# VectorE subtracts a session's upper parts one session later, behind the copy that opens it

## The chip, the cores and the metric

One core of a Trainium2 chip runs the whole program: the matrix engine (TensorE, PE in the rows), VectorE (DVE), ScalarE (ACT), GpSimd (POOL), which here issues transfers, and SyncE (SP), which issues the others. The metric is the time of one execution in microseconds, the median of several runs.

## The reference

Attention through 49 agents for four batches of 12480 tokens, and behind it a two-layer network with squared relu over all 49920 rows:

```
a2k     = softmax(scale * agents @ k.T)        # per batch, 49 x 12480
agent_v = a2k @ v                              # 49 x 128
x       = softmax(scale * q @ agents.T) @ agent_v
h       = maximum(x @ w_in, 0)                 # 49920 x 2048
out     = (h * h) @ w_out                      # 49920 x 128
```

## The kernel before

The kernel never forms x. For each batch it multiplies agent_v with w_in into a table (`aw_hi` and a small rest `aw_ex`), so that a block of at most 504 tokens needs only its softmax weights (`w`, `x`), which are multiplied with the table to give h. The 2048 columns of h are 16 chunks of 128.

**Sessions.** The main loop runs over sessions: 199 that take one block of 504 (or, at a batch's end, 384) tokens and 8 of the 16 chunks, and two of 4 chunks at the very end. A block is two sessions. In session s, TensorE first makes the 8 chunks of h (`first`: 8 matmuls with the table and 8 narrow ones, `x<-` in the rows, which run four at a time on 19 rows). They fill all eight banks of its accumulator memory, four called x and four called y; the tags A and B change places from session to session. ScalarE rectifies 7 banks into a tile `r` of fp32, VectorE the eighth (`rectified`, `r<-A` or `r<-B` on DVE). ScalarE squares `r` in two halves of four chunks (`squared`), and behind each half GpSimd issues a transfer that writes the half's fp16 rounding, the upper part `g_hi` (line 1039).

**Two sessions later** (`LAG`), TensorE multiplies these squares back with w_out (`second`): per chunk `g_hi` with the lower and the upper part of w_out (16 matmuls), and then `g_lo` with the upper part (8 matmuls, `g_lo,wo_hi`). `g_lo = r - g_hi` is the lower part. VectorE makes it, in two subtractions of 128x2016 a session (`rest`, called by `low_parts`). All 24 matmuls add into one bank, x[0] of the running session, and VectorE copies the sums out (`copied_out`, `ob<-`), scaled, adding two sessions to a block's result. I call this the copy. A copy of session n's sums comes at the end of session n+2. The next session needs the bank back for the first of its y chunks: its narrow matmul into that bank waits for the copy.

**What sets the order.** Every instruction of TensorE, ScalarE and VectorE is chained to the one issued before it on its engine, so each engine runs in the order of the program's text. Work for the softmax weights of later blocks, and for keys and values of the next batch, is cut into steps that are called at named phases of a session: L, P, A1, D, E, A3. P holds TensorE's steps; A1 and A3 ScalarE's; D and E VectorE's. In D stand the maximum and the subtraction of a block's scores (`m`, `e`) or the cast of its turned weights (`w`), in E the normalising group (three on `z`, one on `e`), or `pp`, or steps on `mx` and `d` for keys and values.

**Around the change**, VectorE's order within session s is: the eighth bank's rectification, phase D, the first subtraction for session s-1, the copy of session s-2, phase E, the second subtraction for s-1. The function `ending` runs what is left of `second` and the copy; `low_parts` calls it between its two subtractions. At the start (s = 0), nine instructions that split the last quarter of w_out's parts (`makes`, `keeps`: tiles `last`, `t`, `wo_hi`, `wo_lo`) stand behind phase D of session 0. At the end, `late_parts` rounds and subtracts for the two sessions of four chunks, on VectorE alone.

Of the kernel before, what the change touches and what calls it, by code (L numbers as in the profile page):

```python
# [29 lines left out]
LAG = 2  # L30
# [3 lines left out]
WIDE = 512  # L34
# [16 lines left out]
def agent_attention_relu2(ctx: ExitStack, tc: tile.TileContext, qT, kT, v, agT, w_in, w_out, outT):  # L51
# [4 lines left out]
    FF = w_in.shape[1]  # L56
# [15 lines left out]
    def queued(issue, eng, *args, **kw):  # L72

        with tc.issue_after(chain[eng]) if eng in chain else ExitStack():
            ins = issue(*args, **kw)  # L75
        chain[eng] = ins.ins
        return ins
# [75 lines left out]
    def decoded(dec, raw, t):  # L153
        low, high = raw[:, :, 0], raw[:, :, 1]
        n = raw.shape[1]
        dve.scalar_tensor_tensor(
            out=t, in0=high, scalar=0xC0000000, in1=t, op0=ALU.bitwise_and, op1=ALU.bitwise_or
        )

        rest = dec[:, 1, :] if n == 512 and not hasattr(dec, "tile") else dec.tile([P, n], F32, name="rest", bufs=4)  # L160
        dve.tensor_single_scalar(rest.bitcast(U32), t, 0xFF800000, op=ALU.bitwise_and)
        dve.scalar_tensor_tensor(out=rest, in0=low, scalar=2.0**-52, in1=rest, op0=ALU.mult, op1=ALU.mult)
        return t.bitcast(F32), rest

    def kept(at, t, rest):
        n = t.shape[1]
        if at < FF:
            pool.tensor_add(win[:, at : at + n], t, rest)
            if at + n == FF:
                pool.tensor_mul(squares, win, win)  # L170
            return iter(())
        c = slice((at - FF) // C, (at - FF + n) // C)
        hi, lo = (x[:, c, :].rearrange("p c d -> p (c d)") for x in (wo_hi, wo_lo))
        return kept_later(hi, lo, t, rest) if at > FF else scaled(hi, lo, t, rest)
# [306 lines left out]
    def place(k):  # L481
        b, i = divmod(k // HALF, HB)
        return b * NB + i // 2, i % 2, k % HALF * SET

    def width(k):
        return REST if k // HALF % HB == HB - 1 else G
# [58 lines left out]
    def rest(lo, r, hi, at, n):  # L545
        x = slice(at % SET, at % SET + n)
        queued(nc.vector.tensor_sub, nc.vector, lo[:, x, :], r[:, at : at + n, :], hi[:, x, :])
# [4 lines left out]
    def lower(k):  # L552
        return late.tile([P, SET, G], F16, name="g_lo", bufs=LOWS)[:, :, : width(k)]

    def second(k, m, o):
        _, _, at = place(k)
        his, los = parts.pop(k)
        todo = [(w, c, his[c // SET][:, c % SET, :]) for c in range(m * SET) for w in (wo_lo, wo_hi)]
        for x, lo in enumerate(los):
            todo += [(wo_hi, x * SET + c, lo[:, c, :]) for c in range(SET)]  # L560
        last = len(todo) - 1
        for i, (w, c, y) in enumerate(todo):
            queued(nc.tensor.matmul, nc.tensor, o, w[:, at + c, :], y, start=(i == 0), stop=(i == last))
            yield

    def copied_out(k, m, o):
        g, j, at = place(k)
        if at == 0:
            whole[0] = late.tile([P, G], F32, name="ob", bufs=3)[:, : width(k)]
            queued(nc.vector.tensor_scalar_mul, nc.vector, whole[0], o, state[g // NB]["rho"])  # L570
        else:
            queued(
                nc.vector.scalar_tensor_tensor, nc.vector, out=whole[0], in0=o, scalar=state[g // NB]["rho"],
                in1=whole[0], op0=ALU.mult, op1=ALU.add,
            )
        if at + m * SET == NCH:
            t = g // NB * N + (g % NB * 2 + j) * G
            nc.sync.dma_start(outT[:, t : t + width(k)], whole[0])
# [28 lines left out]
    def step(gen):  # L607

        with ExitStack() as es:
            for ins in behind:  # L610
                es.enter_context(tc.issue_after(ins))
            return next(gen, None)

    def run(gen):
        for _ in gen:
            pass
# [51 lines left out]
    with tc.tile_pool(name="pre", bufs=PRE) as pre, tc.tile_pool(name="raws", bufs=RAW) as raws_in, tc.tile_pool(name="dec", bufs=4) as dec:  # L668
# [47 lines left out]
        def makes(at):  # L716
            raws[at] = decoded(*raws[at])

        def keeps(at):
            return kept(at, *raws.pop(at))  # L720
# [19 lines left out]
        for i in range(NK):  # L740
# [7 lines left out]
            s = sp.tile([P, 512], F32, name="s")[:, :n]  # L748
# [8 lines left out]
            if i in (0, 4, 8):  # L757
                at = i // 4 * WIDE
# [39 lines left out]
        z = small.tile([P, 1], F32, name="z0")  # L798
# [96 lines left out]
    sessions, starts, at = [], [], 0  # L895
# [43 lines left out]
    def allowed(name, s, gate):  # L939
        if gate == "told":  # L940
            return s == todo["told"]
        if gate == "any":
            return s >= todo["start"]
        if gate == "values":
            todo["told"] = s + 2 + s % 2
        todo["room"] = room(s if gate == "blocks" else todo["told"])
        return todo["room"] > 0

    def phase(name, s):
        for gen in plan.pop((s, name), ()):  # L950
            step(gen)
        while todo["next"]:
            (at, lead, *gate), since = todo["next"]
            if at != name or s < since + lead or gate and not allowed(name, s, *gate):
                break
            said = step(todo["gen"])
            todo["next"] = said and (said, s)
# [7 lines left out]
            rounded(hi, r, i, 2)  # L965
            rest(lo, r, hi, i, 2)

    def low_parts(z, first):
        k, n = sessions[z]
        r, his = made.pop(z)  # L970
        los = [lower(k) for _ in range(n)]
        parts[k] = his, los
        phase("D", z + 1)
        for x in range(n):
            if x:
                run(first)
                phase("E", z + 1)
            rest(los[x], r, his[x], x * SET, SET)

    def resting(n):  # L980
        for _ in range(n):
            pe.matmul(desk["at"][BLOCKS][:, :P], ones, ones, start=True, stop=True)

    def ending(s, work, o):
        run(work)
        if s >= LAG:
            copied_out(*sessions[s - LAG], o)
        yield

    made, x = {}, None  # L990
    todo["end"] = starts[NB]
    for s in range(len(sessions) + LAG):
        k, m = sessions[s] if s < len(sessions) else (total, 0)
        if s == LAG:
            behind = [chain[eng] for eng in (nc.tensor, nc.sync, nc.scalar, nc.vector, nc.gpsimd)]
        if s in starts and s // 2 and starts.index(s) % NB == 0:
            assert not todo["next"]
            b = starts.index(s) // NB
            if b + 1 < B:
                todo.update(gen=background(b + 1), done=0, start=s, end=starts[(b + 1) * NB])  # L1000
                todo["next"] = (step(todo["gen"]), s)
        phase("L", s)

        tags = "AB" if s % 2 == 0 else "BA"
        x = Banks(tags[0])
        o = x[0][:, : width(sessions[s - LAG][0])] if s >= LAG else None

        if m:
            r = held("r", F32, m, k)
            made[s] = r, []  # L1010
            if s:
                x, y = first(k, m, x, lambda: Banks(tags[1]))
                rectified(r, x, 0)
            else:
                x, _ = first(k, 1, x, None)
                rectified(r, x, 0)
                for n in (2, 3):
                    run(table(n, (n - 1,)))
                y, _ = first(k + 1, 1, Banks(tags[1]), None)
        desk["at"] = x  # L1020
        work = second(*sessions[s - LAG], o) if s >= LAG else iter(())
        for _ in range(LEAD):
            next(work, None)
        if s and s < LAG:
            resting(IDLE[0])
        phase("P", s)
        if s and s < LAG:
            resting(IDLE[1])
        if m == 2:
            rectified(r, y, SET, TAKEN[s] if s < LAG else 1)  # L1030
        if s == 0:
            phase("D", s)
            makes(2 * FF - WIDE)
            for at in (FF + 2 * WIDE, FF + 3 * WIDE):
                run(keeps(at))
        for x in range(m if m == 2 else 0):
            squared(r, x * SET, SET)
            made[s][1].append(upper(x, k))
            nc.gpsimd.dma_start(made[s][1][x], r[:, x * SET : (x + 1) * SET, :])  # L1039
            if x == 0:  # L1040
                phase("A1", s)
        if m != 2:
            phase("A1", s)
        if m == 1:
            for n in (0, 2):
                squared(r, n, 2)
        ended = ending(s, work, o)
        if s - 1 in made:
            low_parts(s - 1, ended)
        phase("D", s)  # L1050
        run(ended)
        phase("E", s)
        if m == 1:
            late_parts(s)
        phase("A3", s)
        todo["more"]()
# [36 lines left out]
```

## Time and profile before

| | us |
|---|---|
| median of 3 runs | 1760.4 (1758.71 to 1764.08) |
| the profiled execution, its own time | 1757.98 |
| its span | 1755.8 |
| TensorE busy | 1691.0 (96%) |
| VectorE busy | 1478.8 (84%) |
| ScalarE busy | 1499.9 (85%) |
| share of full clock that TensorE was granted | 0.995 |

A busy engine is one whose instructions overlap any moment; matmuls are pipelined, so TensorE's busy time counts their modelled tails too. A wait in the rows is idle time of one engine just before an instruction, with what released it in square brackets. In a timeline row the first number is the start, the second the duration, both in us; `x8` means that eight equal instructions are merged.

### The profile page before, as it was taken

The numbers are of one execution on the slowest core, as the hardware profiler recorded it, in microseconds if no ns is written. First come the engines' busy times: TensorE is split into PE (matmuls) and PEld (weight loads), VectorE is DVE, ScalarE is ACT, GpSimd is POOL, SyncE is SP. The second block draws the span as 40 slices with busy tenths as digits, with TensorE's granted clock in tenths as the row PEclk, the third lists the DMA queues.
The fourth block names the chain that finished last, engine by engine and source line by source line (L and its number), as shares of the span: only waits on it lengthen the run. The fifth ranks groups of instructions, "written<-read, shape, count | busy, mean of one in ns | idle before, by whom it ended". The sixth has DMA issues, their size and how long they took to land.

```text
span 1755.8 us, 40344 instructions
## 1 busy us (share of the span) xinstructions
PE 1691.0 (96%) x16731; PEld 788.0 (45%) x16731; DVE 1478.8 (84%) x1602; ACT 1499.9 (85%) x2063; POOL 233.4 (13%) x422
## 2 busy tenths in 40 slices
PE   7799999999999999999999999999999999999998
PEld 3444444444444444444444444444444444444444
DVE  6888878888887788888888788888888888888887
ACT  4688888888888888988889789888888999999996
POOL 2211111111111111111111111111111111111111
PEclk9999999999999999999999999999999999999999
DMA  9678888889788888888779887888778888787776
GB/s 380 182 172 197 211 185 186 200 193 205 161 172 183 210 185 193 193 201 187 160 166 189 191 192 168 178 208 187 153 158 167 177 170 186 165 175 166 155 156 122
DMA packets 116439, 324.03 MB, mean 185 GB/s; under 512 B 13648, under 2 KB 48160, under 8 KB 116256
## 3 DMA queue, kind: packets, MB, share of 16 engines
q0 software_dynamic: 62688, 203.71, 60.7%
q1 hardware_dynamic: 53568, 117.74, 20.5%
q8 instruction: 131, 2.15, 0.5%
q14 instruction: 52, 0.43, 0.1%
HBM read 80.97 MB, written 25.56 MB: 61 GB/s over the span
## 4 chain that ended last, share of the span: by engine, by line
PE 50%; issue 33%; DMA 5%; DVE 5%; POOL 4%; ACT 3%; SPq 0%; POOLq 0%; ACTq 0%; DVEq 0%
PE A L75 26%; PE B L75 23%; DMA g_hi<-r 4%; POOL g_hi L1039 4%; ACT r L75 2%; DVE g_lo L75 1%; DMA ahead<-in_kT 1%; DVE ob L75 1%; PE h L75 1%; PE o L75 0%; DVE e L75 0%; DVE r L75 0%; DVE z L75 0%; POOLq L1039 0%; SPq L75 0%
## 5 line engine op out<-in xcount | busy, mean ns | idle before, releaser
L75 DVE TENSOR_TENSOR g_lo<-r,g_hi 128x2016 f16<-128x2016 f32 (+2 forms) x402 | 892.2, 2220 | 67.5 <-DMA g_hi<-r 66.8
L75 ACT ACTIVATE r<-r 128x2016 f32<-128x2016 f32 (+2 forms) x402 | 742.6, 1916 | 1.3 <-DVE r L75 1.3
L75 ACT ACTIVATE r<-B 128x504 f32<-128x504 f32 (+1 forms) x698 | 359.4, 611 | 137.1 <-PE B L75 136.9
L75 PEld LDWEIGHTS <-wo_hi 128*128 128x128 f16 x3200 | 313.1, 98 | 354.2 <-issue 16.1
L75 ACT ACTIVATE r<-A 128x504 f32<-128x504 f32 (+1 forms) x699 | 360.2, 614 | 67.3 <-PE A L75 67.2
L1039 POOL DMA_DIRECT2D g_hi<-r x398 | 213.7, 537 | 1453.7 <-ACT r L75 1366.3
L75 PE MATMUL A<-g_hi,wo_lo 128*128 128x504 f16 (+1 forms) x804 | 303.0, 377 | 1.5 <-issue 0.8
L75 PE MATMUL A<-g_hi,wo_hi 128*128 128x504 f16 (+1 forms) x804 | 302.0, 376 | 0.0
L75 PE MATMUL B<-g_hi,wo_lo 128*128 128x504 f16 (+1 forms) x796 | 298.0, 374 | 0.6 <-ACT r L75 0.6
L75 PE MATMUL B<-g_hi,wo_hi 128*128 128x504 f16 (+1 forms) x796 | 297.6, 374 | 0.0
L75 PEld LDWEIGHTS <-aw_hi 128*128 128x128 f16 x1600 | 140.4, 98 | 215.5 <-issue 78.8
L75 PEld LDWEIGHTS <-wo_lo 128*128 128x128 f16 x1600 | 156.6, 98 | 171.0 <-issue 6.9
L75 PE MATMUL A<-w,aw_hi 128*128 128x504 f16 (+1 forms) x800 | 219.1, 376 | 2.8 <-DVE r L75 2.8
L75 PE MATMUL B<-w,aw_hi 128*128 128x504 f16 (+1 forms) x800 | 220.2, 378 | 1.6 <-DVE aw_hi L75 1.6
L75 PE MATMUL A<-g_lo,wo_hi 128*128 128x504 f16 (+1 forms) x804 | 186.4, 374 | 6.3 <-issue 5.4
L75 PE MATMUL B<-g_lo,wo_hi 128*128 128x504 f16 (+1 forms) x796 | 184.1, 374 | 0.0
L75 DVE TENSOR_SCALAR ob<-A,rho 128x504 f32<-128x504 f32 (+1 forms) x100 | 73.7, 737 | 82.3 <-PE A L75 54.8
L75 DVE SCALAR_TENSOR_TENSOR ob<-B,rho,ob 128x504 f32<-128x504 f32 (+1 forms) x100 | 73.4, 734 | 36.3 <-PE B L75 33.3
L75 PE MATMUL B<-x,aw_ex 19*128 19x504 f16 (+1 forms) x800 | 77.9, 376 | 18.5 <-DVE ob L75 17.8
L75 PE MATMUL A<-x,aw_ex 19*128 19x504 f16 (+1 forms) x800 | 77.0, 375 | 5.2 <-DVE ob L75 5.2
L75 PEld LDWEIGHTS <-aw_ex 19*128 19x128 f16 x1600 | 28.1, 92 | 119.6 <-issue 119.1
L75 DVE CAST w<-B 98x504 f16<-98x504 f32 (+1 forms) x97 | 65.3, 673 | 10.7 <-ACT r L75 10.2
(192 smaller groups left out, 1004.3 us busy)
## 6 DMA issues: line engine op xcount, KB each, us to landing
g_hi<-r POOLq DMA_DIRECT2D x384, 504.0 KB, 7.0
qt<-in_qT SPq DMA_DIRECT2D x48, 504.0 KB
out_T<-ob SPq DMA_DIRECT2D x96, 252.0 KB
vt<-in_v SPq DMA_DIRECT2D x36, 512.0 KB
kt<-in_kT SPq DMA_DIRECT2D x36, 512.0 KB
x<-w SPq DMA_DIRECT2D x384, 18.7 KB
ahead<-in_kT SPq DMA_DIRECT2D x12, 512.0 KB
ahead<-in_v SPq DMA_DIRECT2D x12, 512.0 KB
```

The source lines that it names most:

```text
L75: ins = issue(*args, **kw)
L1039: nc.gpsimd.dma_start(made[s][1][x], r[:, x * SET : (x + 1) * SET, :])
```

## The change

`low_parts` loses its second argument and the calls between its subtractions. It is called two sessions after the session whose parts it makes, right after the first chunks of the running session are issued, instead of one session after, in front of phase D. `ending` is gone: phase D, then phase E, then the rest of `second` and the copy. The splitting of w_out's last quarter moves from session 0 to session 1, behind phases D and E.

```diff
-    def low_parts(z, first):
+    def low_parts(z):
         k, n = sessions[z]
         r, his = made.pop(z)
         los = [lower(k) for _ in range(n)]
         parts[k] = his, los
-        phase("D", z + 1)
         for x in range(n):
-            if x:
-                run(first)
-                phase("E", z + 1)
             rest(los[x], r, his[x], x * SET, SET)
...
-    def ending(s, work, o):
-        run(work)
-        if s >= LAG:
-            copied_out(*sessions[s - LAG], o)
-        yield
...
         desk["at"] = x
+        if s - LAG in made:
+            low_parts(s - LAG)
         work = second(*sessions[s - LAG], o) if s >= LAG else iter(())
...
         if s == 0:
             phase("D", s)
-            makes(2 * FF - WIDE)
-            for at in (FF + 2 * WIDE, FF + 3 * WIDE):
-                run(keeps(at))
...
-        ended = ending(s, work, o)
-        if s - 1 in made:
-            low_parts(s - 1, ended)
         phase("D", s)
-        run(ended)
         phase("E", s)
+        if s == 1:
+            makes(2 * FF - WIDE)
+            for at in (FF + 2 * WIDE, FF + 3 * WIDE):
+                run(keeps(at))
+        run(work)
+        if s >= LAG:
+            copied_out(*sessions[s - LAG], o)
         if m == 1:
             late_parts(s)
```

No instruction is added or removed. TensorE, ScalarE and GpSimd keep their order row for row; SyncE's transfers of weights change places with a neighbour here and there; VectorE's order changes.

**A session in the steady part**, VectorE, before, from one copy (`ob`) over the next to the one after. The first subtraction stands in front of the copy, the normalising group and the second subtraction behind it:

```order
L75 TENSOR_SCALAR r<-A_2658 128x504
L75 CAST w_2697<-B_2649 98x504
L75 TENSOR_TENSOR g_lo<-r,g_hi_2607 128x2016
L75 SCALAR_TENSOR_TENSOR ob<-B_2646,rho_785,ob 128x504
L75 TENSOR_REDUCE z<-e 126x8
L75 TENSOR_SCALAR z<-z 126x8
L75 RECIPROCAL z<-z 126x8
L75 TENSOR_TENSOR e<-e,z 126x392
L75 TENSOR_TENSOR g_lo<-r,g_hi_2612 128x2016
L75 TENSOR_SCALAR r<-B_2746 128x504
```

And now:

```order
L75 TENSOR_SCALAR r<-A_2654 128x504
L75 CAST w_2695<-B_2645 98x504
L75 TENSOR_REDUCE z<-e 126x8
L75 TENSOR_SCALAR z<-z 126x8
L75 RECIPROCAL z<-z 126x8
L75 TENSOR_TENSOR e<-e,z 126x392
L75 SCALAR_TENSOR_TENSOR ob<-B_2642,rho_785,ob 128x504
L75 TENSOR_TENSOR g_lo<-r,g_hi_2607 128x2016
L75 TENSOR_TENSOR g_lo<-r,g_hi_2612 128x2016
L75 TENSOR_SCALAR r<-B_2742 128x504
```

The first subtraction (of the same tile, g_hi_2607) went behind the copy, and the group on `z` in front of it.

**The start**, VectorE, sessions 0 to 2, before: the splitting of w_out stands ahead of the group on `z` and of session 1's rectification (`r<-A`), the subtractions for session 0 right behind phase D's `e`:

```order
L75 SCALAR_TENSOR_TENSOR wo_lo<-last,omega 128x512
L75 TENSOR_REDUCE z<-e 126x8
...
L75 TENSOR_SCALAR r<-A_910 128x504
L75 TENSOR_TENSOR pp<-e,pp 126x8x49
L75 TENSOR_REDUCE m<-B_900 126x8
L75 TENSOR_TENSOR e<-B_900,m 126x392
L75 TENSOR_TENSOR g_lo<-r,g_hi_892 128x2016
```

And now:

```order
L75 TENSOR_SCALAR r<-A_901 128x504
L75 TENSOR_TENSOR pp<-e,pp 126x8x49
L75 TENSOR_REDUCE m<-B_891 126x8
L75 TENSOR_TENSOR e<-B_891,m 126x392
L75 SCALAR_TENSOR_TENSOR last<-raw_last,last 128x512
...
L75 SCALAR_TENSOR_TENSOR wo_lo<-last,omega 128x512
L75 TENSOR_TENSOR g_lo<-r,g_hi_883 128x2016
```

The nine splitting instructions now stand between phase D of session 1 and the subtractions for session 0.

**The end**, VectorE, before: `g_lo<-r,g_hi_21003` and `21006` are the subtractions for the last session of eight chunks, `g_hi_21081` belongs to the first of the two late ones:

```order
L75 TENSOR_TENSOR g_lo<-r,g_hi_21003 128x4x384
L75 SCALAR_TENSOR_TENSOR ob<-B_21032,rho_16109,ob 128x504
L75 TENSOR_TENSOR g_lo<-r,g_hi_21006 128x4x384
L75 CAST g_hi_21081<-r 128x2x384
L75 TENSOR_TENSOR g_lo<-r,g_hi_21081 128x2x384
...
L75 TENSOR_SCALAR ob<-A_21087,rho_16109 128x384
```

And now:

```order
L75 SCALAR_TENSOR_TENSOR ob<-B_21028,rho_16107,ob 128x504
L75 CAST g_hi_21077<-r 128x2x384
L75 TENSOR_TENSOR g_lo<-r,g_hi_21077 128x2x384
...
L75 TENSOR_TENSOR g_lo<-r,g_hi_21003 128x4x384
L75 TENSOR_TENSOR g_lo<-r,g_hi_21006 128x4x384
L75 TENSOR_SCALAR ob<-A_21083,rho_16107 128x384
```

Both subtractions went behind the copy and behind the four instructions of the first late session.

## Rows read from the trace of the kernel before

**Rows 1.** Page: busy us, share of the span, instructions.

```profile
PE 1691.0 (96%) x16731; PEld 788.0 (45%) x16731; DVE 1478.8 (84%) x1602; ACT 1499.9 (85%) x2063; POOL 233.4 (13%) x422
```

**Rows 2.** Waits of TensorE: total us, times, longest us.

```profile
PE B L75 <- DVE ob L75: 17.8, 24, 1.2
...
PE A L75 <- DVE ob L75: 5.2, 6, 1.2
```

**Rows 3.** Waits of VectorE, same columns.

```profile
DVE g_lo L75 <- DMA g_hi<-r: 66.8, 54, 2.7
...
DVE aw_lo L75 <- ACT aw_hi L75: 17.0, 10, 2.7
```

**Rows 4.** Timeline of VectorE, 214 to 233 us: start, duration, instruction, wait.

```profile
214.56 0.74 DVE L75 TENSOR_SCALAR ob<-A,rho 128x504 f32<-128x504 f32 x1 [1.20 <-PE A L75]
...
221.89 2.26 DVE L75 TENSOR_TENSOR g_lo<-r,g_hi 128x2016 f16<-128x2016 f32 x1 [2.71 <-DMA g_hi<-r]
224.07 0.73 DVE L75 SCALAR_TENSOR_TENSOR ob<-B,rho,ob 128x504 f32<-128x504 f32 x1
...
232.83 0.74 DVE L75 TENSOR_SCALAR ob<-A,rho 128x504 f32<-128x504 f32 x1 [1.59 <-ACT pp L75]
```

**Rows 5.** Timeline of VectorE, 1042 to 1061 us, the same pair of sessions.

```profile
1042.87 0.74 DVE L75 TENSOR_SCALAR ob<-A,rho 128x504 f32<-128x504 f32 x1 [2.07 <-PE A L75]
...
1046.81 0.68 DVE L75 CAST w<-B 98x504 f16<-98x504 f32 x1
...
1050.58 0.74 DVE L75 SCALAR_TENSOR_TENSOR ob<-B,rho,ob 128x504 f32<-128x504 f32 x1
1051.24 0.55 DVE L75 TENSOR_REDUCE z<-e 126x8 f32<-126x392 f32 x1
...
1052.82 2.25 DVE L75 TENSOR_TENSOR g_lo<-r,g_hi 128x2016 f16<-128x2016 f32 x1
1054.98 0.68 DVE L75 TENSOR_SCALAR r<-B 128x504 f32<-128x504 f32 x1
...
1059.72 0.74 DVE L75 TENSOR_SCALAR ob<-A,rho 128x504 f32<-128x504 f32 x1 [1.90 <-issue]
```

**Rows 6.** Timelines of TensorE and ScalarE, 1042 to 1051 us.

```profile
1042.67 1.01 PE L75 MATMUL B<-w,aw_hi 128*128 128x504 f16 x4
...
1044.05 0.38 PE L75 MATMUL A<-x,aw_ex 19*128 19x504 f16 x4
...
1048.68 1.86 PE L75 MATMUL B<-g_lo,wo_hi 128*128 128x504 f16 x8
...
1047.56 3.71 ACT L75 ACTIVATE r<-r 128x2016 f32<-128x2016 f32 x2
```

**Rows 7.** Timelines of VectorE and ScalarE at the start, 76 to 97 us.

```profile
76.28 0.68 DVE L75 SCALAR_TENSOR_TENSOR last<-raw_last,last 128x512 uint32<-128x512 uint32 x1
...
91.20 0.67 DVE L75 TENSOR_SCALAR r<-B 128x504 f32<-128x504 f32 x1
...
93.89 2.25 DVE L75 TENSOR_TENSOR g_lo<-r,g_hi 128x2016 f16<-128x2016 f32 x1
96.06 0.73 DVE L75 TENSOR_SCALAR ob<-A,rho 128x504 f32<-128x504 f32 x1
...
77.31 0.52 ACT L75 ACTIVATE e<-e 126x392 f32<-126x392 f32 x1
...
80.08 1.92 ACT L75 ACTIVATE r<-r 128x2016 f32<-128x2016 f32 x1
```

**Rows 8.** Timelines of VectorE and TensorE at the end, 1742 to 1752 us.

```profile
1742.94 1.75 DVE L75 TENSOR_TENSOR g_lo<-r,g_hi 128x1536 f16<-128x1536 f32 x1
...
1746.28 1.46 PE L75 MATMUL A<-g_lo,wo_hi 128*128 128x384 f16 x8
...
1748.37 0.55 DVE L75 CAST g_hi<-r 128x768 f16<-128x768 f32 x1
...
1751.29 0.61 DVE L75 SCALAR_TENSOR_TENSOR ob<-B,rho,ob 128x384 f32<-128x384 f32 x1
```

## The prediction

> **What bounds the kernel now.** I read the page's busy times first: TensorE is busy for 1691.0 us, 96% of the span [rows 1]. So only TensorE's own waits can be won back, and the next view is the list of what it waits for. The first cause behind the start is the copy of sums: 17.8 us in 24 waits and 5.2 us in 6, the longest 1.2 us [rows 2], together 23.0 us in 30. The reader is to see that these are not one wait per session but 30 in 200 sessions. Why these 30? VectorE's list answers: 54 times, 66.8 us in all, it stood before a subtraction until the transfer of an upper part had landed [rows 3]. VectorE runs in order, so the copy queued behind that subtraction stood too.
>
> A pair of sessions shows it. From the copy at 214.56 to the next at 224.07 pass 9.51 us, because the first subtraction waited 2.71 us for its transfer; the copy after that starts at 232.83, 8.76 us later [rows 4]. The same two kinds of session without a harmful wait take 7.71 and 9.14 us [rows 5]. The first copy of the pair was therefore 9.51 - 7.71 = 1.80 us late, and the pair lost 18.27 - 16.85 = 1.42 us. Two things follow. TensorE forgives a copy that is up to 1.80 - 1.42 = 0.38 us late: undisturbed, the narrow matmul that needs the bank starts at 1044.05 [rows 6], 0.44 us after the copy's end at 1043.61 [rows 5]. And such a wait costs more than the list says: the longest there is 1.2 us [rows 2], and this one cost 1.42. I take 0.2 us more per wait, since a matmul's modelled tail covers part of the gap.
>
> **What the change does to a steady session.** It moves subtractions, and adds none. Between two copies VectorE now runs both subtractions, the eighth bank, phase D, phase E, and the next copy. Nothing of this waits for a fresh transfer: in the slow pair the awaited transfer had landed at 221.89, 2.18 us before the copy at 224.07 [rows 4]. With that copy on time (1.80 earlier, 222.27) and the subtraction 0.66 us behind it (copy to next instruction, 1050.58 to 1051.24 [rows 5]), it would start at 222.93, still 1.04 us after the landing, and this was the longest of the 54 waits. So I cost the transfer's wait at nothing, with 1.04 us of cover.
>
> *Does TensorE get the lower parts in time?* Counted from a copy's start C = 1042.87 [rows 5]: the first subtraction starts at C + 0.66 and takes 2.25, ready at C + 2.91; the second starts 2.16 after the first (1052.82 to 1054.98) and is ready at C + 5.07. TensorE takes the lower parts at 1048.68 [rows 6], C + 5.81, the second four matmuls 0.9 us later (half of the eight's 1.86). Cover 2.9 and 1.6 us: nothing.
>
> *Does the next copy come in time?* The tightest session is the one with a cast in D and the group on `z` in E: 50 of the 201 stretches between copies in the new order. Its sum, from starts to next starts where the rows have them: copy 0.66, two subtractions 2 x 2.16, eighth bank at most 0.68, cast at most 0.68, group 1052.82 - 1051.24 = 1.58 [rows 5]: 7.92 us. TensorE needs 7.71, so the copy is 0.21 late at most, inside the 0.38 that is forgiven: nothing, but the cover is only 0.17 us. These instructions start 0.08 or 0.09 us before their forerunners have ended (a subtraction of 2.25 is followed after 2.16, a copy of 0.74 after 0.66 [rows 5]). The Trainium skill, page "VectorE: DVE Perf Modes", section "Terms", says that the pipe is flushed after every VectorE operation and the next cannot issue before it is empty; added up end to end, the durations of the same rows would give some 8.2 us a session, and 50 sessions would lose about 0.1 us each. The trace does not agree: it shows the overlap, and I take 7.92.
>
> *What of the gain stays away?* Where VectorE waits for ScalarE's part of a new table (`aw_lo`, 17.0 us in 10 waits [rows 3]), the copy stays late if a normalising group now stands in front of it as well. I leave 1.2 us of gain to these, three waits of 0.4. Bounds: 0, and 3 us if three copies stay as late as the longest.
>
> Steady sum: 30 waits, 23.0 us, plus 30 x 0.2 = 6.0, less 1.2, less 0.5 for one that lies at the start: **-27.3 us**. Lower bound of the gain, the list alone less 3: 20. Upper: 29.
>
> **The start.** The nine splitting instructions move behind VectorE's phase D of session 1, ahead of session 0's subtractions. VectorE's work up to these subtractions is the same, now with two waits in it: the `z` group comes at 76.28 and needs the exponential that ScalarE ends at 77.31 + 0.52 = 77.83, 1.55 us; and `pp` needs a cast that ScalarE can only begin after its square, at 80.08 + 1.92 = 82.00, and that takes about 0.5 (my estimate, from the exponential of the same tile, 0.52): 82.5, where VectorE would arrive at 77.83 + 1.58 + 3 x 0.6 = 81.2: 1.3 us. The stretch that ended at 91.20 ends at 94.05; then eighth bank, cast and group, 93.89 - 91.20 = 2.69 as before, and the copy at 96.74 instead of 96.06 [rows 7]. **+0.7 us**, since the next session's narrow matmul waits for this copy. TensorE gets session 1's banks earlier than before, but now waits for the lower parts, so I credit nothing. Bounds: -2, if the earlier banks carry through, and +4, if TensorE after this idling runs slowly for some us.
>
> **The end.** The subtractions for the last session of eight chunks stood before and behind the copy that ends at 1742.94; now both follow it, and the four instructions of the first late session stand between (they take 1751.29 - 1748.37 = 2.92 us, as the second late session's). VectorE: 1742.94 + 2.92 + 2 x 1.7 = 1749.26; TensorE needs that second lower part, which it took from 1746.28 on; its last four matmuls take 0.7 (half of 1.46), the copy 0.5, the last late session 2.92: 1753.4 where it was 1751.29 [rows 8]. **+2.1 us.** Nothing hides it, as every step waits for the one before; bounds 1.5 and 3.
>
> **Sum:** -27.3 + 0.7 + 2.1 = -24.5 us. Against the profiled execution: 1757.98 - 24.5 = 1733.5. The median of the runs shown is 1760.4, 2.4 us above that execution, so 1735.9; I say 1736.
>
> **The rivals.**
> *VectorE becomes the bound in the 50 tight sessions.* For it: cover of 0.17 us. Against: the sum has two durations in it where the true pitch is shorter. At 0.2 us a session beyond the cover it costs 10 us: 1746. By the Trainium skill's flush, in the section named above, it would be 1741.
> *The transfers land later.* They move the same bytes in less time; if one lands more than 1.04 us later than in [rows 4], the wait now opens the session and holds both subtractions and the copy. If it takes back most of the gain: 1757, no change. Against: a transfer has a whole session more.
> *Slower: the eighth bank.* Its rectification now stands behind both subtractions. It starts at C + 0.66 + 2 x 2.16 = C + 4.98 and ends at C + 5.66 = 1048.53. ScalarE's second square needs it and starts at about 1047.56 + 1.86 = 1049.42 [rows 5, 6]. Cover 0.89 us. It decides from there: every 0.1 us beyond, in 199 sessions, is up to 20 us as soon as ScalarE has no idle time left; 0.12 us beyond eats the gain, and 0.2 us gives 1776, slower. Against it: only a wait in front of the subtractions could bring it, and none is left that I see.
> *The new order isn't what it says,* because some wait ties the subtractions to the old place: nothing in the order shows one; 1760.
>
> **How the numbers follow.** Forecast 0.80; tight sessions 0.08; transfers 0.04; eighth bank 0.05; no effect 0.03. A measurement can tell about 0.3%, 5 us, from no change, so faster means under 1755: the first two cases and a little of the third, 0.88; same 0.06; slower 0.06. The forecast's own range: the steady gain 20 to 29, start -2 to +4, end 1.5 to 3 give at the extremes 1760.4 - 29.5 = 1731 and 1760.4 - 13 = 1747; with 2 us for the median's scatter below and the tight sessions above I give 1729 to 1750.
>
> **What would show it.** Right: VectorE's wait for the transfer of `g_hi` gone or under 5 us; TensorE's waits for `ob` at 1 to 3 us instead of 23.0; tight sessions at 7.71 us from copy to copy; the copy at the start near 96.7; the end some 2 us longer from the last full copy. Wrong: waits of TensorE for `ob` in sessions with a group on `z`, or for `g_lo`; ScalarE's square waiting for `r` from VectorE; a wait for the transfer in front of the first subtraction behind a copy.

## The result and the profile after

The change makes the kernel faster by 1.65%: 1730.8 us (median of 4 runs, 1726.9 to 1734.0) against 1759.6 us for the kernel before on the same chip, a ratio of 0.9835 with a 95% interval of 0.9802 to 0.9868. The forecast was 1736 us with a range of 1729 to 1750. The result lies inside the range, near its lower end. A second measurement on another occasion (`e11_after_again`) gave 1730.6 against 1760.9 us, 0.9820 (0.9792 to 0.9848). The profiled execution of after took 1732.19 us, its span is 1730.1 us, 25.7 us less than before's.

The same instructions run, and TensorE's share of the span is one point higher than in [rows 1]. Its busy time is 5.7 us less; the section on the prediction takes that up:

```profile
PE 1685.3 (97%) x16731; PEld 785.7 (45%) x16731; DVE 1467.7 (85%) x1602; ACT 1500.1 (87%) x2063; POOL 234.3 (14%) x422
```

The waits of all engines in after (engine, what it is about to do, what released it: us in total, times, longest us) answer to [rows 2, 3]:

```profile
DVE mx L75 <- ACT s L75: 30.6, 32, 2.9
...
PE A L75 <- issue: 12.5, 9, 3.3
...
ACT r L75 <- DVE r L75: 7.9, 7, 5.1
...
DVE aw_lo L75 <- ACT aw_hi L75: 6.7, 7, 1.4
...
PE A L75 <- DVE g_lo L75: 6.1, 4, 2.9
...
DVE g_lo L75 <- DMA g_hi<-r: 0.7, 1, 0.7
...
PE B L75 <- DVE ob L75: 0.5, 1, 0.5
```

Read it from below. TensorE waited 23.0 us in 30 waits for the copy (`ob`); it now waits once, 0.5 us. VectorE waited 66.8 us for the fresh upper part (`g_hi`); it now waits 0.7 us once. What is new stands in the middle: TensorE waits four times for a lower part (`g_lo`), twice at the start and twice at the end, and ScalarE once 5.1 us for VectorE's eighth bank, at the start. The first line is idle time of VectorE, which reaches phase E earlier and waits there for ScalarE; no wait of TensorE in after is put down to `mx`, so it costs nothing.

The tight session, the one with a cover of only 0.17 us in the prediction, in VectorE's timeline of after (start, duration, instruction, wait; it answers to [rows 5]):

```profile
1021.16 0.74 DVE L75 TENSOR_SCALAR ob<-A,rho 128x504 f32<-128x504 f32 x1 [2.41 <-PE A L75]
1021.82 4.42 DVE L75 TENSOR_TENSOR g_lo<-r,g_hi 128x2016 f16<-128x2016 f32 x2
1026.15 0.68 DVE L75 TENSOR_SCALAR r<-A 128x504 f32<-128x504 f32 x1
1026.75 0.67 DVE L75 CAST w<-B 98x504 f16<-98x504 f32 x1
1027.34 0.55 DVE L75 TENSOR_REDUCE z<-e 126x8 f32<-126x392 f32 x1
...
1028.37 0.57 DVE L75 TENSOR_TENSOR e<-e,z 126x392 f32<-126x392 f32 x1
1028.87 0.74 DVE L75 SCALAR_TENSOR_TENSOR ob<-B,rho,ob 128x504 f32<-128x504 f32 x1
```

From copy to copy it takes 1028.87 - 1021.16 = 7.71 us, with VectorE busy throughout. That is what TensorE needs too, so VectorE is just full in these sessions.

**Where the 25.7 us lie.** Take the programme in four stretches, bounded by rows of VectorE that both kernels have:

| stretch | before us | after us | difference |
|---|---|---|---|
| to the first `r<-B` of three banks (starts at 73.36, 74.45) | 73.36 | 74.45 | +1.1 |
| from there to the second copy (103.35, 106.68) | 29.99 | 32.23 | +2.2 |
| from there to the last full copy (1742.28, 1714.13) | 1638.93 | 1607.45 | -31.5 |
| from there to the last copy of all (1752.01, 1726.26) | 9.73 | 12.13 | +2.4 |

The first line is loading, which the change doesn't touch; it varies between profiles whatever the order (a kernel with before's order, `e1_landed` below, started 1.4 us later than before). The other three are the prediction's steady part, start and end.

The steady gain lies in the first three of the four batches. From the copy at 1378.78 in before (1350.68 in after) to the last full copy, which is nearly all of the last batch, the two kernels take 363.50 and 363.45 us, though VectorE still waits there 23 times for a transfer in before, by up to 1.40 us. TensorE's last wait for a copy in before is at 1327.91. The last batch has no next batch's keys and values to prepare; that this is why its waits do no harm was not tried.

At the start VectorE's rows in after, which answer to [rows 7], are these:

```profile
83.54 0.57 DVE L75 TENSOR_TENSOR pp<-e,pp 126x392 f16<-126x392 f32 x1 [1.22 <-ACT pp L75]
...
85.10 0.68 DVE L75 SCALAR_TENSOR_TENSOR last<-raw_last,last 128x512 uint32<-128x512 uint32 x1
...
90.92 4.42 DVE L75 TENSOR_TENSOR g_lo<-r,g_hi 128x2016 f16<-128x2016 f32 x2
...
97.95 0.74 DVE L75 TENSOR_SCALAR ob<-A,rho 128x504 f32<-128x504 f32 x1
```

and TensorE's:

```profile
93.22 1.09 PE L75 MATMUL A<-g_lo,wo_hi 128*128 128x504 f16 x4 [2.91 <-DVE g_lo L75]
95.39 1.84 PE L75 MATMUL A<-g_lo,wo_hi 128*128 128x504 f16 x4 [1.08 <-DVE g_lo L75]
97.03 1.88 PE L75 MATMUL B<-w,aw_hi 128*128 128x504 f16 x4
```

The nine splitting instructions (from 85.10) stand between session 0's data and its subtractions (from 90.92). TensorE waits 2.91 and 1.08 us, and then its matmuls are slow: four wide ones take 1.88 us where they take 1.01 elsewhere [rows 6]. This profile's start is the longest of those taken of it: two other kernels with the same start, `e11_after_again` and `e5_end_early`, need 31.59 and 31.55 us to the second copy, so the start costs 1.6 to 2.2 us.

At the end, in VectorE's timeline of after (for [rows 8]), the four instructions of the first late session stand in front of the last two subtractions of eight chunks; the merged row holds the late session's last one, of 0.96 us, and these two:

```profile
1714.13 0.74 DVE L75 SCALAR_TENSOR_TENSOR ob<-B,rho,ob 128x504 f32<-128x504 f32 x1 [1.67 <-issue]
...
1716.83 4.29 DVE L75 TENSOR_TENSOR g_lo<-r,g_hi 128x768 f16<-128x768 f32 x3
1722.09 0.62 DVE L75 TENSOR_SCALAR ob<-A,rho 128x384 f32<-128x384 f32 x1 [0.96 <-issue]
```

VectorE idles 1.67 us in front of the full copy, and the subtractions that could fill this gap are queued behind it.

### The profile page after: what moved, and what is told of

Its sections match the earlier page's. It is cut to its first block, busy times and chain, and to the rows that moved or that the text cites. A ratio compares the mean times of both kernels' runs of the same rounds, so it can differ in the third digit from the quotient of the medians.

```text
span 1730.1 us, 40279 instructions
## 1 busy us (share of the span) xinstructions
PE 1685.3 (97%) x16731; PEld 785.7 (45%) x16731; DVE 1467.7 (85%) x1602; ACT 1500.1 (87%) x2063; POOL 234.3 (14%) x422
## 5 line engine op out<-in xcount | busy, mean ns | idle before, releaser
L75 DVE TENSOR_TENSOR g_lo<-r,g_hi 128x2016 f16<-128x2016 f32 (+1 forms) x402 | 875.8, 2220 | 0.8 <-DMA g_hi<-r 0.7
L75 DVE TENSOR_SCALAR r<-B 128x504 f32<-128x504 f32 (+1 forms) x102 | 68.2, 671 | 1.1 <-PE B L75 1.1
L75 DVE TENSOR_SCALAR r<-A 128x504 f32<-128x504 f32 (+1 forms) x101 | 67.7, 672 | 0.0
```

## The experiments

The theory: the copy came late because a subtraction that waited for a fresh transfer stood in front of it; everything else in the diff costs a little at both ends. Rivals: the place of phase E, in front of the copy, is what helps; or one of the covers in the prediction isn't there. All runs are shown against the kernel before on the same chip:

| kernel | median us | before us | ratio (95% interval) |
|---|---|---|---|
| after | 1730.8 | 1759.6 | 0.9835 (0.9802 to 0.9868) |
| e1_landed | 1738.8 | 1758.3 | 0.9901 (0.9876 to 0.9926) |
| e9_landed_ahead | 1733.0 | 1758.8 | 0.9848 (0.9814 to 0.9881) |
| e2_group_first | 1792.4 | 1758.3 | 1.0200 (1.0169 to 1.0232) |
| e3_group_behind | 1742.8 | 1758.3 | 0.9921 (0.9896 to 0.9946) |
| e8_three_more | 1735.1 | 1758.3 | 0.9880 (0.9856 to 0.9905) |
| e4_split_early (one execution) | 1730.1 | 1758.8 | |
| e5_end_early (one execution) | 1729.5 | 1758.8 | |
| e11_after_again | 1730.6 | 1760.9 | 0.9820 (0.9792 to 0.9848) |
| e6_both_ends | 1727.2 | 1760.9 | 0.9809 (0.9783 to 0.9834) |
| e10_split_spread | 1723.0 | 1760.9 | 0.9788 (0.9763 to 0.9814) |

### Is it the transfer's wait?

Before, with one operand exchanged:

```diff
+        landed[z] = his
+        old = landed.get(z - 1)
+        if not old or width(sessions[z - 1][0]) != width(k):
+            old = his
...
-            rest(los[x], r, his[x], x * SET, SET)
+            rest(los[x], r, old[x], x * SET, SET)
```

> The order of before, unchanged in every row; only what the two subtractions read is changed: the upper part of the session before, which landed a session ago, in place of the fresh one (so the lower parts are those of another tile). Theory (the fresh transfer's wait is the whole cause): VectorE's wait of 66.8 us for the transfer and TensorE's 23.0 us for the copy both go to under 3 us, and the time falls by 27 to 32 us, to 1728 to 1733, without any new order. Rival (the order counts: the group on z in front of the copy is what lets the copy come in time): TensorE goes on waiting for the copy for some 15 us or more, 1750 to 1760.

The waits in it:

```profile
PE A L75 <- DVE ob L75: 4.1, 5, 1.2
...
PE B L75 <- DVE ob L75: 3.2, 4, 1.2
...
DVE g_lo L75 <- DMA g_hi<-r: 1.7, 3, 0.8
```

Neither theory had it right. The wait for the transfer is gone, and 19.5 us with it, without any new order; that is two thirds of the gain and rules out the rival. But TensorE still waits 7.3 us for the copy, in nine waits where there were 30. They lie in and around the sessions that make a new table, and there the transfer had not been the cause: the ten copies around the second of these tables take 77.28 us in before (836.67 to 913.95) and 77.28 us in e1_landed (822.55 to 899.83). VectorE's timeline of e1_landed shows one:

```profile
853.60 0.74 DVE L75 SCALAR_TENSOR_TENSOR aw_lo<-A,rl,aw_hi 49x512 f16<-49x512 f32 x1 [2.66 <-ACT aw_hi L75]
854.26 2.24 DVE L75 TENSOR_TENSOR g_lo<-r,g_hi 128x2016 f16<-128x2016 f32 x1
856.43 0.73 DVE L75 TENSOR_SCALAR ob<-A,rho 128x504 f32<-128x504 f32 x1
```

VectorE waits 2.66 us for ScalarE's `aw_hi`, and only then makes a subtraction whose data have long been there, and the copy stands behind both: 10.06 us from the copy at 846.37 to this one. The same session in after:

```profile
846.54 4.41 DVE L75 TENSOR_TENSOR g_lo<-r,g_hi 128x2016 f16<-128x2016 f32 x2
...
852.92 0.74 DVE L75 SCALAR_TENSOR_TENSOR aw_lo<-A,rl,aw_hi 49x512 f16<-49x512 f32 x1 [1.37 <-ACT aw_hi L75]
853.98 0.74 DVE L75 TENSOR_SCALAR ob<-A,rho 128x504 f32<-128x504 f32 x1 [0.32 <-PE A L75]
```

Both subtractions are made while ScalarE works, the wait is 1.37 us, the copy comes in time: 8.09 us from the copy at 845.89.

So the next kernel is e1_landed with the first subtraction in front of phase D, where `aw_lo` stands:

```diff
-        phase("D", z + 1)
         for x in range(n):
             if x:
+                phase("D", z + 1)
                 run(first)
```

> As e1_landed (before's text, the subtractions read the landed upper part of the session before, so the lower parts are those of another tile), and the first subtraction goes in front of phase D instead of behind it: eighth bank, first subtraction, D, copy, E, second subtraction. Theory (what e1_landed still lacked, some 9 us, is lost in the sessions that make a new table, where VectorE waits up to 2.7 us for ScalarE's aw_hi and then has a subtraction of 2.16 us between aw_lo and the copy): TensorE's waits for the copy fall from 7.4 us to under 3 us, the three stretches of table sessions get 2 us shorter each, and the time falls by 6 to 10 us, to 1729 to 1733. Rival (these sessions need the group on z in front of the copy, or both subtractions behind it): TensorE's waits for the copy stay over 6 us, 1737 to 1741.

It ran 25.9 us faster than before, 6.3 us better than e1_landed. The intervals of the two just overlap, so the stretch of table sessions decides: from the copy at 821.98 to the one at 896.66 it takes 74.68 us, against 77.28 in e1_landed and 75.10 in after. The theory's time holds. Its count of waits does not quite:

```profile
DVE g_lo L75 <- DMA g_hi<-r: 12.7, 5, 3.4
...
PE B L75 <- DVE ob L75: 3.6, 3, 1.4
...
PE A L75 <- DVE ob L75: 1.7, 3, 0.7
```

TensorE's waits are 5.3 us, not under 3. The three of 3.6 us belong to the experiment: at a batch's end the width of the tiles changes, no landed tile fits, and the kernel falls back to the fresh one, for which VectorE now waits up to 3.4 us. With that said, two things make nearly the whole steady gain (from the second copy to the last full one, e9_landed_ahead takes 1610.5 us, after 1607.5 and before 1638.9): a subtraction no longer waits for its transfer in front of the copy, and no longer stands between `aw_lo` and the copy.

### Does the place of phase E help by itself?

Before, with phase E called in front of the copy instead of behind it, nothing else:

```diff
             if x:
-                run(first)
                 phase("E", z + 1)
+                run(first)
```

> The order of before with phase E alone moved in front of the copy: D, first subtraction (which still waits for its transfer), E, copy, second subtraction. Theory: the wait stays in front of the copy and E's 1.58 us is added behind it, so TensorE's waits for the copy grow from 23.0 us to 40 us or more, and VectorE's wait for the transfer stays over 60 us; 1765 to 1800. Rival (moving E is where the gain comes from): TensorE's waits for the copy fall below 10 us, 1730 to 1745.

It is 34 us slower than before. Its waits:

```profile
DVE g_lo L75 <- DMA g_hi<-r: 49.2, 60, 1.9
...
PE B L75 <- DVE ob L75: 38.6, 37, 2.7
...
PE A L75 <- DVE ob L75: 1.9, 3, 0.8
```

TensorE's waits for the copy grow from 23.0 to 40.5 us, as the theory said. The wait for the transfer fell to 49.2 us, where I had expected it above 60; a VectorE that arrives later at the subtraction would do that, but it was not tried.

The 17.5 us more of waiting are only about half of the loss. Much of the rest is TensorE's clock. The four runs were granted 0.983 to 0.988 of it, the seven of before on this chip 0.992 to 0.995. In the profile, behind a wait of 1.98 us for the copy at 526.85, single wide matmuls take 0.63 us, where they take 0.38 at full clock. Added up over stretches of 4 us, the clock that was not granted in the steady part comes to 13.7 us in this kernel and 1.7 us in before.

This part of the diff, alone, is the slower case; it pays only when the waiting subtraction is out of the way.

### Is there cover for the eighth bank?

After, with phase E back behind the copy, so in front of the subtractions and of the eighth bank:

```diff
-        phase("E", s)
...
             copied_out(*sessions[s - LAG], o)
+        phase("E", s)
```

> The order of after, with phase E put back behind the copy: copy, E, two subtractions, eighth bank, D, copy. Theory (my cover of 0.89 us for the eighth bank): in the 50 sessions with a group on z, 1.58 us, the eighth bank ends about 0.7 us after ScalarE's second square could begin, so ScalarE waits for r from VectorE some 50 times, 30 to 40 us in all against 7.9; ScalarE has idle time, so TensorE loses less: 1732 to 1750. Rival (the place of E is indifferent): ScalarE's waits for r from VectorE stay under 12 us, 1728 to 1733.

It costs 12 us against after (by the ratios 15). ScalarE waits for VectorE's bank 48 times:

```profile
ACT r L75 <- DVE r L75: 30.8, 48, 5.1
```

One of these sessions, VectorE:

```profile
1601.31 0.55 DVE L75 TENSOR_REDUCE z<-e 126x8 f32<-126x392 f32 x1
...
1602.88 4.42 DVE L75 TENSOR_TENSOR g_lo<-r,g_hi 128x2016 f16<-128x2016 f32 x2
1607.22 0.67 DVE L75 TENSOR_SCALAR r<-B 128x504 f32<-128x504 f32 x1
```

and ScalarE's second square, which takes the bank:

```profile
1605.33 1.94 ACT L75 ACTIVATE r<-r 128x2016 f32<-128x2016 f32 x1
1607.99 1.88 ACT L75 ACTIVATE r<-r 128x2016 f32<-128x2016 f32 x1 [0.71 <-DVE r L75]
```

The group puts 1.57 us in front of the bank and the square is 0.71 late, so the cover in after is 0.86 us; the prediction had 0.89. In 43 sessions of the last batch, where TensorE is busy all the time in after and ScalarE 93% of it, the loss goes through whole: 341.5 us from copy to copy instead of 334.8. The rival of the prediction that ended slower was a real edge, 0.9 us away.

### How full are the tight sessions?

After, with three small instructions behind phase E of every session:

```diff
         phase("E", s)
+        for _ in range(3):
+            dve.tensor_scalar_mul(filler, filler, 1.0)
```

> The order of after, with three more small VectorE instructions (128x8, about 0.2 us each, 0.6 us in all, on a tile that nothing else uses) behind phase E in every session. Theory: the 50 tight sessions, whose VectorE work from copy to copy takes 7.71 us where TensorE needs 7.71, come 0.6 us late, 0.38 of it is forgiven, TensorE waits 0.2 us for the copy in each: 10 us, 1738 to 1745. Rival (there is more slack than the copy shows, since a late copy is made up in the next session): under 3 us, 1729 to 1734. Other rival (nothing is forgiven): 30 us, 1755 to 1765.

It took 1735.1 us, a ratio 0.0045 to 0.006 above after's two (its interval overlaps one of theirs), between my theory and the first rival. VectorE's timeline shows why:

```profile
1021.36 0.74 DVE L75 TENSOR_SCALAR ob<-A,rho 128x504 f32<-128x504 f32 x1 [1.47 <-PE A L75]
...
1029.05 0.58 DVE L75 TENSOR_SCALAR filler<-filler 128x8 f32<-128x8 f32 x3
1029.54 0.74 DVE L75 SCALAR_TENSOR_TENSOR ob<-B,rho,ob 128x504 f32<-128x504 f32 x1
...
1038.24 0.74 DVE L75 TENSOR_SCALAR ob<-A,rho 128x504 f32<-128x504 f32 x1 [0.39 <-PE A L75]
```

The three take 1029.54 - 1029.05 = 0.49 us, not 0.6. The tight session grows from 7.71 to 8.18 us, and the next one shrinks from 1037.95 - 1028.87 = 9.08 to 8.70 (the first two numbers are copies of after): 0.38 us of the lateness is forgiven, as the prediction said, and 0.09 are lost in each of these pairs, 4.5 us in 50 of them. The theory of the edge holds; I had its size from a wrong price. VectorE has no slack in these sessions, and TensorE forgives 0.38 us.

### The start and the end

After with the splitting back in session 0:

```diff
         if s == 0:
             phase("D", s)
+            makes(2 * FF - WIDE)
+            for at in (FF + 2 * WIDE, FF + 3 * WIDE):
+                run(keeps(at))
```

> After, with the nine splitting instructions of w_out's last quarter back in session 0. Theory (their new place delays session 0's subtractions; TensorE waits 2.9 and 1.1 us for them and then runs at half its clock for some 4 us): TensorE's waits for g_lo at the start fall from 4.0 us to under 1 us, its clock is not cut behind them, and the second copy (block 0 complete) ends 2 to 3 us earlier, counted from VectorE's first r<-B of 1.86 us (after: 74.45 to 107.34, 32.9 us; before: 73.36 to 104.01, 30.65 us): 30 to 31 us. Rival (the splitting only fills VectorE's waits for ScalarE, so the early place costs as much): 32.5 us or more.

From the `r<-B` row to the second copy it takes 105.04 - 74.93 = 30.11 us (to its end 30.8), against 32.23 in after (31.55 and 31.59 in the other two profiles of that start). TensorE's waits for lower parts at the start are gone. Its clock is cut here too, though, earlier, behind a wait of 2.4 us for VectorE's `r`, as it was in before. That part of the expectation failed. A cut at that place does no visible harm: 30.11 us here and 29.99 in before.

After with the last two subtractions around the copy of the session before:

```diff
-        if s >= LAG:
+        if s == len(sessions) - 2:
+            low_parts(s - 1, lambda: copied_out(*sessions[s - LAG], o))
+        elif s >= LAG:
             copied_out(*sessions[s - LAG], o)
```

> After, with the two subtractions for the last session of eight chunks put back around the copy of the session before (one in front of it, one behind it) and so in front of the first late session's four instructions. Theory: TensorE's waits for g_lo at the end (1.2 and 0.9 us) go, and from the end of the copy of the last 504-token block's second session to the last copy it takes 9.6 us as in before, not 12.0. Rival (the waits only move to another place of the closing chain): 11.5 us or more.

VectorE at the end of this kernel:

```profile
1707.77 6.08 DVE L75 TENSOR_TENSOR g_lo<-r,g_hi 128x2016 f16<-128x2016 f32 x3
1713.86 0.74 DVE L75 SCALAR_TENSOR_TENSOR ob<-B,rho,ob 128x504 f32<-128x504 f32 x1
...
1723.59 0.62 DVE L75 SCALAR_TENSOR_TENSOR ob<-A,rho,ob 128x384 f32<-128x384 f32 x1
```

One subtraction (the third of the merged row) now fills the gap in front of the full copy. From that copy to the last it takes 1723.59 - 1713.86 = 9.73 us, before's time exactly; after's 12.13 came from this.

Then both together, and a third place for the splitting, with after once more beside them:

> After, unchanged, as the yardstick of the next two on the same chip: 1728 to 1734 by every theory.

> After with both repairs: the nine splitting instructions back in session 0, and the last subtractions back around the copy of the session before. Theory (the two costs are separate and add): the second copy starts 30 to 30.5 us after VectorE's first r<-B of 1.86 us starts (after: 32.2) and the end takes 9.6 us (after: 12.0), 4 to 5 us less than after, 0.25%: ratio to before about 0.981. Rival (what is won at one end is lost elsewhere): the same as after.

> After with the end repaired as in e6_both_ends, and the splitting spread: its first three instructions in session 0, where VectorE waits 1.5 us for ScalarE's exponential, the next three behind phase E of session 1, the last three behind the first copy. Theory (VectorE's queue is what the start waits for, and only the first three lie in a wait): the second copy starts 28 to 29.5 us after VectorE's first r<-B, 3 to 4 us earlier than after, and the whole takes 5 to 6.5 us less than after: ratio about 0.980. Rival (the last three, now between the first copy and the subtractions behind it, hold back the second copy as long as the others did): 30 us or more.

e10_split_spread is after with the end of e5_end_early and this:

```diff
         if s == 0:
             phase("D", s)
+            makes(2 * FF - WIDE)
...
         phase("E", s)
-        if s == 1:
-            makes(2 * FF - WIDE)
-            for at in (FF + 2 * WIDE, FF + 3 * WIDE):
-                run(keeps(at))
+        if s == 1:
+            run(keeps(FF + 2 * WIDE))
...
+        if s == LAG:
+            run(keeps(FF + 3 * WIDE))
```

e6_both_ends: 1727.2 us, 3.3 less than after beside it; 30.11 us at the start and 9.7 at the end, as expected. Its interval overlaps after's, so that it is faster rests on these two stretches, which the profile times. e10_split_spread: 1723.0 us, 7.6 less than after beside it; the two intervals overlap here too, but four of after's five runs (1724.4 to 1732.0) took longer than all four of this kernel (1722.1 to 1725.5). Its rows:

```profile
73.77 1.86 DVE L75 TENSOR_SCALAR r<-B 128x504 f32<-128x504 f32 x3 [1.10 <-PE B L75]
...
101.74 0.74 DVE L75 SCALAR_TENSOR_TENSOR ob<-B,rho,ob 128x504 f32<-128x504 f32 x1
```

27.97 us to the second copy, 3.6 less than after in the profile beside it (4.3 less than in the first) and 2.0 less than before. The first three instructions fill VectorE's wait for ScalarE, and of the other six TensorE notices little: its longest wait for VectorE there is 0.95 us. Of the 7.6 us the two stretches explain 3.6 + 2.4 = 6.0; the rest is not accounted for.

## Why the prediction was right, point by point

*The wait and the copy.* Right. TensorE's waits for `ob` were to fall to 1 to 3 us and fell to 0.5; the transfer's wait was to fall under 5 us and fell to 0.7. No transfer lands late enough to matter.

*The steady part, -27.3 us.* Too small: -31.5 in this pair of profiles. Two rows split it, before's steady stretch and after's (stretch, its length, then busy us and instructions of TensorE, its weight loads, VectorE, ScalarE, GpSimd, then the granted clock, DMA share, GB/s):

```profile
103.35:1742.28 1638.93, 1600.95 (x15940) 738.43 (x15939) 1389.83 (x1445) 1436.96 (x1951) 209.79 (x391) 1.00 0.83 181
106.68:1714.13 1607.45, 1592.72 (x15940) 734.41 (x15939) 1379.07 (x1446) 1437.03 (x1951) 210.64 (x391) 1.00 0.84 185
```

TensorE's idle time falls from 37.98 to 14.73 us, by 23.25; the sum had 23.0 - 0.5 - 1.2 = 21.3 for it. The step "What of the gain stays away?" is the larger part of the difference: it left 1.2 us in the sessions that wait for `aw_lo`, because a group on `z` would stand in front of the copy there. The rows of after and e9_landed_ahead show the opposite: with the subtractions out of the gap between `aw_lo` and the copy, these sessions win, and one 0.5 us wait is all that is left.

The same 15940 matmuls are busy for 8.23 us less. The sum had 6.0 for that, the 0.2 us per wait for modelled tails; "only TensorE's own waits can be won back" was too narrow. Some 1.7 us of the 8.23 are a stretch of before at a cut clock (983 to 991 us), behind a stall of 2.19 us that no copy caused: luck. The other 6.5 make 0.22 us per wait, but how much of them is tails isn't shown: in six profiles with after's steady order this busy time runs from 1592.7 to 1596.4 us, and the whole stretch from 1604.1 to 1608.9. Of before there is one profile.

*The thin cover in the tight sessions.* The danger was named, the sum was off: 7.92 us by adding rows, 7.71 in the trace. Adding the whole of the eighth bank's 0.68 and the cast's 0.68 was the cause; their pitch is 0.60 and 0.59 (1026.15, 1026.75, 1027.34). The group's is 1.53, not 1.58. So the copy isn't late at all, and 0.38 us is left, not 0.17; e8_three_more used it up. The Trainium skill's rule of a flush after each operation (page "VectorE: DVE Perf Modes", section "Terms") would have cost these sessions 0.1 us each by the prediction's estimate. The trace does not agree: here the copy starts at 1028.87, 0.07 us before the group's last row ends (1028.37 + 0.57), and the session takes TensorE's 7.71 us.

*The start, +0.7 us.* Too small: +2.2 in this profile, +1.6 in two others of the same start. The two waits on VectorE (1.55 and 1.3 predicted) are there with 1.49 and 1.22 us, and the first copy came as worked out: 97.95 less the 1.1 us of later loading is 96.86, predicted 96.74. What failed is the sentence "I credit nothing" for TensorE. It was done early, waited 4.0 us for the lower parts and then ran slowly behind the first copy, so that the second followed after 106.68 - 97.95 = 8.73 us where it took 7.29 in before. The 4 us at the upper bound named this; I had taken the middle.

*The end, +2.1 us.* Right in mechanism, measured +2.4: VectorE's way up to the last subtraction's end is as worked out, 1721.12 - 1714.13 = 7.0 us from the full copy, but TensorE's share between this and the copy at 1722.09 is 0.96 us where I had 0.7.

*The eighth bank.* Cover 0.89 us predicted, 0.86 measured by e3_group_behind; the rival stayed away because nothing waits in front of the subtractions any more.

The forecast of 1736 came out 5.2 us above the median. The steady gain was sized too small by 4.2 us and the losses at both ends by 1.8 us together, so that the errors hid each other in part. That the sum against the profiled execution, 1733.5, missed its 1732.19 (with 1.1 us of later loading in it) by only 1.3 us is luck.

## What to carry to other kernels

On an in-order engine, look at what stands right in front of the instruction that frees a resource for the bottleneck engine: work that waits for a transfer or for another engine belongs behind it (here `r` is held one session longer for that, in the same number of buffers), and work that is ready belongs into the wait. The same reordering that is free in the steady state is paid for in the first and the last rounds, where nothing is there to hide it, so those want their own places. A group of instructions that is harmless at one place of the queue (phase E in front of the copy) costs some 12 us behind it, and 34 us in front of it while the wait is still there: test the parts of a reordering together and apart.

## What the runs showed of the hardware

**A wait that costs twice.** One stretch of the start, by windows (stretch in us, its length, busy us and instructions of each engine, then the clock granted to TensorE as a share of full speed, DMA share, GB/s). After:

```profile
96.00:100.00 4.00, 4.00 (x16) 1.02 (x14) 3.90 (x7) 1.99 (x2) 0.53 (x1) 0.50 0.25 53
```

and e10_split_spread:

```profile
96.00:100.00 4.00, 4.00 (x22) 1.90 (x21) 4.00 (x3) 2.88 (x4) 0.53 (x1) 1.00 0.42 79
```

In after TensorE is idle for 2.91 and 1.08 us and is then granted half its clock (the lower level, 1.2 GHz) from 96 to 100 (0.54 in its second profile); behind the short waits of e10_split_spread, up to 0.95 us, it keeps all of it. Before and e4_split_early have such a cut too, 0.69 and 0.50 from 88 to 92, behind a wait of 2.4 us; in after it falls between the first and the second copy, and there it costs time that no sum of waits shows. e2_group_first shows the same in the steady part.

**Stalls that belong to no kernel.** In every profile TensorE loses some microseconds to "issue", waits for which nothing in the trace is given: 12.5 us in 9 stalls in after, up to 3.3 us, 8.7 in 10 in the second profile of the same kernel, 5.9 in 8 in e8_three_more. All nine in after lie in sessions with a step for keys or values, five of them within the runs of narrow 128x49 matmuls. Before has 12.6 us in 10. They are part of the scatter between profiles, some 5 us in the steady stretch, and of what a comparison of two profiles can show; what they are was not tried.
